# Seven half-block products in place of eight for the second FFN product of chunks 2 to 8

## The chip, the cores and the metric

The kernel runs on one core of a Trainium2 chip. A core has five engines with an instruction queue each: TensorE (PE in the profile; PEld are its weight loads), VectorE (DVE), ScalarE (ACT), GpSimd (POOL) and SyncE (SP), which here only issues DMAs. The engines work side by side and wait for each other by semaphores. Matmul results land in PSUM, eight banks of 512 f32 values in each of 128 partitions; everything else lies in SBUF.

The metric is the device time of one execution in microseconds, the median of several runs. Less is better.

## The reference

An attention with 8 batches, 8 heads, 576 positions and 64 dimensions a head, in which half of the heads see a plain window of 32 positions ("plain") and half see every fourth of the last 128 ("dilated"); its output, as 4608 tokens of 512 values, goes through a gated FFN:

```python
def _moe_ref(x, w_gate, w_val, w_out):
    g = x @ w_gate                                   # 4608 x 512 @ 512 x 1536
    gelu = 0.5 * g * (1.0 + erf(g * inv_sqrt2))
    val = x @ w_val
    return (gelu * val @ w_out).astype(np.float32)   # 4608 x 1536 @ 1536 x 512
```

Inputs and output are f32; the kernel multiplies in f16 and accumulates in f32.

## The kernel before

The 4608 tokens are worked off in nine chunks of 512 tokens, c = 0 to 8. Each has two stages.

The **gate stage** computes, for twelve blocks nb of 128 columns of d_ff, the gate product and the value product (ffn1_part, L617, 4 matmuls of 512 columns each) into two pairs of PSUM banks that alternate; from chunk 2 on blocks with even nb use banks 0 and 7, those with odd nb 1 and 4. ScalarE makes g = gelu(gate) (L776), VectorE u = USCALE * g * value (L781), written as block nb of the tile u_all (128 x 12 x 512, f16).

The **out stage** is the second product, u @ w_out: for four blocks of 128 tokens twelve matmuls of 512 columns (ffn2, L624), into banks 0 and 7 in turn in chunks 1 to 6. Each result is evicted by VectorE or ScalarE with a factor 1/USCALE (store, L635 and L637) to one of four buffers osb and stored by a DMA issued on SP (L639). The fourth of a chunk (e3) is evicted by ScalarE at the head of the next gate stage. The very last block of the kernel is cut in 384 and 128 columns (last_block, L648 to L660).

In chunks 1 to 6 the attention of the next batch is woven into the out stage, four head pairs i, j, k, l of it. Per pair: S, the scores, on TensorE (L452); P, the exponentials, on ScalarE (L482); M, the mask, on VectorE (L487); D and N, denominator and numerator, on TensorE (L452); l and r, the reciprocal by logarithm and exponential, on ScalarE (L579, L585); X, numerator times reciprocal into xT, on VectorE (L608). xT is what the gate stages of the next chunks read. For batches 2 and 3 the dilated pairs are i and j, for later ones k and l.

GpSimd turns loaded f32 into f16: for a batch the casts of q and k (cast_plain L211, cast_dil L223) and of v (cast_v L248, called by cast_part). The inputs of a batch are loaded on SP two chunks ahead: load_first loads q and k and emits their casts; load_rest emits DMA transposes (turn, L266) and the loads of v (load_v, L235 to L244). The v casts of batches 5 to 7 are emitted by the words v0 and v1 in the out stage, behind a mask (word M); those of batch 4 by load_rest(4) itself.

The order on every engine is written out by hand: gate_words(c) and out_words(c) give a string of words, run_program emits them one after the other, and each engine takes its instructions in that order. A number n emits the next n matmuls of the stage's product; g and u the two steps of a block; e and w evictions; F, H and R loads (F b is load_first(b), H b is load_rest(b), R stands at the head of chunk 2's gate stage and is load_rest(3), load_first(4), load_rest(4)); E and G load ScalarE's tables. The list of matmuls of a gate stage starts with an order by hand (orders, firsts), in which the parts that need the last X of the batch come at the tenth place from chunk 3 on.

Of the kernel before, what the change touches and what calls it, by code (L numbers as in the profile page):

```python
# [9 lines left out]
F16 = mybir.dt.float16  # L10
F32 = mybir.dt.float32
AF = mybir.ActivationFunctionType
ALU = mybir.AluOpType
# [1 line left out]
SYNC = mybir.DependencyInfo(mybir.DependencyClass.Sync, mybir.DependencyReason.DATA)  # L15
WIN = 32
DIL = 4
USCALE = 32.0


@with_exitstack
def kernel(
# [10 lines left out]
    nc = tc.nc  # L33
    B, H, S, D = q.shape
    NT, DM = out.shape
    DFF = moe_w_gate.shape[1]
    P = 128
# [49 lines left out]
    s16 = const.tile([P, 4608], F16, tag="s16")  # L87

    u_all = const.tile([P, NNB, CH], F16, tag="u")

    ps = psum.tile([P, 8, 512], F32, tag="ps")
    psf = ps.rearrange("p b c -> p (b c)")
# [472 lines left out]
            emit_tiles((mms, odd(n)))  # L565

    def two_t(n):
        dt = nrm.tile([P, 18, 32], F32, tag="dt", bufs=1)
        c0 = tiles["den", n]
        nc.vector.transpose(dt.rearrange("p b c -> p (b c)"), psf[:, c0 : c0 + S])  # L570
        rc = nrm.tile([P, 18], F32, tag="rc")
        nc.vector.reciprocal(rc, dt[:, :, 0:1].rearrange("p b c -> p (b c)"))
        tiles["rc", n] = rc
# [64 lines left out]
        t0 = c * CH + tb * P  # L638
        nc.sync.dma_start(out=out[t0 : t0 + P, :], in_=osb)  # L639

    def last_block(c, tb, bank):

        osb = osbp.tile([P, DM], F32, tag="osb")
        t0 = c * CH + tb * P
        for half in range(2):
            cs = slice(384 * half, 384 + 128 * half)
            for fc in range(NNB):
                nc.tensor.matmul(  # L648
                    ps[:, bank + 2 * half - 2, cs],
                    u_all[:, fc, tb * P : (tb + 1) * P],  # L650
                    wo_t[fc // 4][:, fc % 4, cs],
                    start=(fc == 0),
                    stop=(fc == NNB - 1),
                )
            src = ps[:, bank + 2 * half - 2, cs]
            if half:
                nc.vector.tensor_scalar(osb[:, cs], src, 1.0 / USCALE, None, ALU.mult)  # L657
            else:
                nc.scalar.activation(osb[:, cs], src, AF.Copy, bias=0.0, scale=1.0 / USCALE)
            (nc.scalar if half else nc.sync).dma_start(out=out[t0 : t0 + P, cs], in_=osb[:, cs])  # L660

    def warm(n, bank, rows=P, cols=CH):

# [60 lines left out]
    def gate_banks(c, nb):  # L724
# [21 lines left out]
    def out_list(c, banks):  # L746
        order = [(tb, fc) for tb in range(4) for fc in range(NNB)]
        if c == 0:
            order[: 3 * NNB] = [(tb, 4 * i + fc) for i, tbs in enumerate((range(3), range(3), (2, 1, 0))) for tb in tbs for fc in range(4)]
        return [lambda tb=tb, fc=fc: ffn2(c, tb, banks[tb], fcs=(fc,)) for tb, fc in order]  # L750

    def out_banks(c):
        if c == 0:
            return (0, 1, 2, 1)
        return (0, 7, 0, 7) if c < 7 else (2, 3, 5, 6)

    def run_program(c, words, mms, banks):
# [3 lines left out]
        for word in words.split():  # L761
# [20 lines left out]
            elif kind in "ew":  # L782
                at = args[1] if len(args) > 1 else c
                store(at, args[0], out_banks(at)[args[0]], "act" if kind == "e" else "dve")
            elif kind == "L":
                mms.clear()
                last_block(c, 3, banks[3])
# [18 lines left out]
    def gate_words(c):  # L806
# [7 lines left out]
            )  # L814
        loads = {1: "F3", 2: "R", 3: "F5 H5", 4: "F6 H6", 5: "F7 H7"}.get(c, "")
        rest = " ".join(f"4 g{nb} 4 u{nb}" for nb in range(2, NNB - 1))
        if c == 1:
            return f"{loads} 8 G 3 g0 1 u0 3 g1 1 u1 {rest} 4 g{NNB - 1} 4"
        before = f"e3@{c - 1}" if c < NCH - 1 else ""
        return f"{before} {loads} 7 G 3 g0 1 u0 1 g1 4 u1 {rest} 4 g{NNB - 1} 4" + (f" u{NNB - 1}" if c > 6 else "")  # L820

    def out_words(c):

# [8 lines left out]
        v0, v1 = (" v0", " v1") if 2 < c < 6 else ("", "")  # L832
        first = f"1 u11 4 S{i}@1+S{j}@4 E P{i} P{j} M{i} M{j} 7 w0 5" if c < 3 else f"E P{i} P{j} 1 u11 M{i} M{j}{v0} 12 w0 3"
        after = f"S{l + 1}@12+S{l + 2}@15" if 1 < c < 6 else ""
        return (
# [49 lines left out]
```

## Time and profile before

| what | value |
|---|---|
| median of 3 runs | 327.05 us (326.82 to 327.45) |
| profiled execution, first to last instruction (span) | 325.3 us |
| granted TensorE clock, mean | 1.000 |
| out stage of chunk 3 (144.9 to 158.2 us): TensorE, VectorE, ScalarE, GpSimd busy | 13.30, 7.83, 9.12, 2.29 us |
| gate stage of chunk 4 (158.2 to 178.9 us): the same | 20.70, 8.60, 8.98, 5.40 us |
| DMA issues to out_dram on SP | 35 of 256 KB and one of 192 KB |

The profile gives for its own execution the span alone; what a timed run has around its first and last instruction is the difference between the two, 1.75 us by the median.

Line numbers (L624) are those of the kernel before. A row of a group reads: line, engine, operation, output <- inputs, shapes and types, count, then busy time in all and the mean of one in ns, then the engine's idle time just before these instructions and what ended it. A row of the timeline reads: start, length (us), engine, line, operation, count, and in brackets the idle time before it and its releaser. In the timeline a row can merge several instructions. SPq is the issue of a DMA on SP's queue. A matmul row's length contains the pipeline's fill; its pace is the distance of starts.

### The profile page before, as it was taken

To read this page: it belongs to the slowest core of one execution; us is meant where nothing else is said; L and a number is where in the kernel's file an instruction comes from. 1 tells how busy PE (TensorE), PEld (TensorE's weight loads), DVE (VectorE), ACT (ScalarE), POOL (GpSimd) and SP (SyncE) were. 2 spreads that over 40 slices of the span, in tenths; PEclk is the share of its full clock that TensorE was granted. 3 is DMA by queue.
4 is the path that set the end of the run, shared out by engine and by line. 5 is a ranking of instruction groups with operands and counts; after the bars stand their busy time and mean duration, and the time that the engine had idled before them with its cause. 6 is when DMAs were issued, how large, how long until landed. Compare 5 with 4: busy or idle time off the path is not lost.

```text
span 325.3 us, 7737 instructions
## 1 busy us (share of the span) xinstructions
PE 318.9 (98%) x3207; PEld 155.8 (48%) x3207; DVE 150.2 (46%) x226; ACT 159.6 (49%) x240; POOL 82.3 (25%) x134
## 2 busy tenths in 40 slices
PE   6999999999999999999999999999999999999996
PEld 4754544445444445445444544445444544444443
DVE  6864636444644464346533554355434644204410
ACT  2662577435753556346633863376435753233321
POOL 8785603402482512332033201411000000000000
PEclk9999999999999999999999999999999999999999
DMA  8999998988799999897489537972000200020002
GB/s 190 188 188 206 201 191 165 269 180 199 171 271 208 240 169 245 197 222 191 119 201 232 141 104 157 253 173 90 32 2 8 94 33 0 2 99 30 0 34 97
DMA packets 106659, 47.11 MB, mean 145 GB/s; under 512 B 83584, under 2 KB 102144, under 8 KB 106624
## 3 DMA queue, kind: packets, MB, share of 16 engines
q1 hardware_dynamic: 93120, 38.29, 50.0%
q0 software_dynamic: 12944, 7.67, 16.7%
q10 hardware_dynamic: 560, 0.66, 0.7%
q8 instruction: 25, 0.41, 0.6%
q14 instruction: 10, 0.08, 0.1%
HBM read 37.75 MB, written 9.44 MB: 145 GB/s over the span
## 4 chain that ended last, share of the span: by engine, by line
PE 61%; ACT 0%; DVE 0%; issue 0%; ACTq 0%
PE ps L617 38%; PE ps L624 19%; PE ps L452 3%; PE ps L648 1%; ACT lg L579 0%; DVE osb L657 0%; ACTq L579 0%
## 5 line engine op out<-in xcount | busy, mean ns | idle before, releaser
L781 DVE SCALAR_TENSOR_TENSOR u_all<-g,ps 128x512 f16<-128x512 f16 x108 | 74.2, 688 | 110.0 <-PE ps L617 93.3
L776 ACT ACTIVATE g<-ps 128x512 f16<-128x512 f32 x108 | 63.6, 597 | 104.1 <-PE ps L617 104.1
L617 PE MATMUL ps<-xT,wg 128*128 128x512 f16 x432 | 112.5, 379 | 0.3 <-DMA wg<-in_moe_w_gate_dram 0.3
L617 PE MATMUL ps<-xT,wv 128*128 128x512 f16 x432 | 112.3, 379 | 0.0
L624 PE MATMUL ps<-wo,u_all 128*128 128x512 f16 x420 | 96.3, 380 | 0.0
L617 PEld LDWEIGHTS <-wv 128*128 128x128 f16 x432 | 42.1, 98 | 51.1 <-DMA wv<-in_moe_w_val_dram 0.7
L617 PEld LDWEIGHTS <-wg 128*128 128x128 f16 x432 | 42.1, 98 | 50.7 <-DMA wg<-in_moe_w_gate_dram 0.4
L624 PEld LDWEIGHTS <-u_all 128*128 128x128 f16 x420 | 39.1, 98 | 45.5 <-issue 0.5
L608 DVE TENSOR_TENSOR xT<-ps,rb 128x576 f16<-128x576 f32 x32 | 28.8, 938 | 16.9 <-PE ps L452 13.6
L482 ACT ACTIVATE P<-ps 128x832 f16<-128x832 f32 (+1 forms) x32 | 25.3, 835 | 15.4 <-PE ps L452 15.3
L211 POOL CAST s<-stage 128x640 f16<-128x640 f32 x24 | 17.4, 752 | 51.0 <-DMA stage<-in_q_dram 37.9
L248 POOL CAST v<-stage 128x1152 f16<-128x1152 f32 x11 | 12.7, 1151 | 63.0 <-DMA stage<-in_v_dram 47.4
L579 ACT ACTIVATE lg<-ps 128x576 f32<-128x576 f32 x30 | 18.7, 653 | 11.6 <-DVE xT L608 9.0
L637 DVE TENSOR_SCALAR osb<-ps 128x512 f32<-128x512 f32 x22 | 15.1, 686 | 12.2 <-PE ps L624 11.6
L585 ACT ACTIVATE rb<-lg 128x576 f32<-128x576 f32 x30 | 19.5, 690 | 0.3
L635 ACT ACTIVATE osb<-ps 128x512 f32<-128x512 f32 x13 | 7.8, 598 | 21.2 <-PE ps L624 21.2
L223 POOL CAST s<-stage 128x512 f16<-128x512 f32 x24 | 14.4, 627 | 10.1 <-DMA stage<-in_q_dram 7.9
L487 DVE TENSOR_TENSOR P<-P,two_d 128x768 f16<-128x768 f16 x14 | 9.4, 678 | 9.8 <-ACT P L482 9.1
L487 DVE TENSOR_TENSOR P<-P,two_p 128x832 f16<-128x832 f16 x14 | 8.6, 612 | 9.5 <-ACT P L482 9.5
L803 ACT ACT_TABLE_LOAD x9 | 11.5, 1283 | 0.2
L452 PEld LDWEIGHTS <-v 64*64 64x64 f16 x616 | 7.6, 107 | 6.3 <-issue 5.7
L452 PEld LDWEIGHTS <-q 64*64 64x64 f16 x576 | 7.9, 107 | 5.0 <-issue 3.0
(67 smaller groups left out, 135.6 us busy)
## 6 DMA issues: line engine op xcount, KB each, us to landing
out_dram<-osb SPq DMA_DIRECT2D x35, 256.0 KB, 2.8
stage<-in_v_dram SPq DMA_DIRECT2D x28, 144.0 KB, 3.8
stage<-in_q_dram SPq DMA_DIRECT2D x24, 128.0 KB, 3.6
stage<-in_k_dram SPq DMA_DIRECT2D x24, 128.0 KB, 2.9
stage<-in_q_dram SPq DMA_DIRECT2D x6, 512.0 KB, 4.7
stage<-in_k_dram SPq DMA_DIRECT2D x6, 512.0 KB, 5.3
stage<-in_v_dram SPq DMA_DIRECT2D x20, 128.0 KB, 2.8
wo<-in_moe_w_out_dram POOLq DMA_DIRECT2D x3, 512.0 KB, 16.8
```

The lines of the kernel that those rows point to most:

```text
L211: nc.gpsimd.tensor_copy(s16[:, 1280 * t + 640 * g : 1280 * t + 640 * g + 640].rearrange("p (k c) -> p k c", k=5), st_of(i).rearrange("p (k ...
L452: nc.tensor.matmul(o[cols], lhs[rows], rhs[rows], start=st, stop=end, skip_group_check=True)
L482: nc.scalar.activation(pt[:, 0 : src.shape[1]], src, AF.Exp, bias=0.0, scale=scale)
L487: tiles["M"] = nc.vector.tensor_tensor(pt, pt, mask, ALU.mult)
L579: nc.scalar.activation(lg, psf[:, c0 : c0 + S], AF.Ln)
L585: nc.scalar.activation(rb, tiles.pop(("lg", n)), AF.Exp, scale=-1.0)
L608: nc.vector.tensor_tensor(dst, num, rb, ALU.mult)
L617: nc.tensor.matmul(ps[:, bank, :], w[:, kc, ns], xT[kc][:, tok], start=first, stop=end)
L624: nc.tensor.matmul(ps[:, bank, :], u_all[:, fc, tb * P : (tb + 1) * P], wo_t[fc // 4][:, fc % 4, :], start=(fc == 0), stop=(fc == NNB - 1),)
L637: nc.vector.tensor_scalar(osb, ps[:, bank, :], 1.0 / USCALE, None, ALU.mult)
L776: nc.scalar.activation(g, ps[:, gate_banks(c, args[0])[0], :], AF.Gelu)
L781: nc.vector.scalar_tensor_tensor(u_all[:, nb, :], tiles.pop(("g", nb)), USCALE, val, ALU.mult, ALU.mult)
```

## The change

The second product of chunks 2 to 8 is computed by Strassen's scheme. Per pair j of u blocks (2j, 2j+1) and for the two halves of 256 tokens, A is the 2 x 2 arrangement A11, A21 (block 2j, tokens 0 to 255 and 256 to 511), A12, A22 (block 2j+1); B the same of w_out: k = block of the pair, h = half of the 512 output columns. Seven products replace eight: M1 = (A11+A22)(B11+B22), M2 = (A21+A22)B11, M3 = A11(B12-B22), M4 = A22(B21-B11), M5 = (A11+A12)B22, M6 = (A21-A11)(B11+B12), M7 = (A12-A22)(B21+B22). Each is 6 pairs x 2 blocks of 128 tokens = 12 matmuls of 256 columns into one bank.

Word by word: K (weight_sums) makes the sums of w_out once, in chunk 1's gate stage, on VectorE. k (u_sums) makes the sums of u, three instructions per pair, behind every second u word, on VectorE; the differences overwrite u. The products go to two banks in the order M3, M4, M5, M1, M2, M7, M6, where M5 adds to M3's bank, M1 and M7 to M4's. q0, q1, q3 take snapshots M3, M4 and M4+M1 (f32, in SBUF); q2, q4, q5, q6 write the four quarters of the output. s0, s1, s2 (part_sum) are sums between snapshots: f += m3, m3 = q2's quarter - m3, f -= q4's quarter; q5 reads m3, q6 reads f. Their engine is GpSimd in chunks 2 to 7; in chunk 8 s0 and s2 are on VectorE. The number behind the second @ of q and s names the engine (q: 1 ScalarE, 0 VectorE; s: 1 VectorE, 0 GpSimd). The eviction e3 at the head of the next gate stage goes away for these chunks; q6 is emitted at the end of the out stage, ahead of X{l}. The last product is split for the end (last_products). USCALE becomes 16, and the small tile dt of two_t becomes the fixed tile turned, whose place is a snapshot later.

```diff
-USCALE = 32.0
+USCALE = 16.0
...
+    NKP, HM = NNB // 2, DM // 2
+    ux = const.tile([P, NKP, 3, 2 * P], F16, tag="ux")
+    wx = [const.tile([P, 4, 2, HM], F16, tag=f"wx{i}", name=f"wx{i}") for i in range(3)]
+    t3s = [xT[i][:, 0:CH].rearrange("p (j d) -> p j d", j=2) for i in range(3)]
+    turned = const.tile([P, 18 * 32], F32, tag="turned")
+    snap = [vdiag.bitcast(F32)[:, DM * i : DM * i + DM] for i in range(2)] + [turned[:, 0:DM]]
...
-        dt = nrm.tile([P, 18, 32], F32, tag="dt", bufs=1)
+        dt = turned.rearrange("p (b c) -> p b c", c=32)
...
+    def weight_sums(i, part):
+        w = wo_t[i].rearrange("p (j k) (h d) -> p j k h d", k=2, h=2)
+        b11, b12, b21, b22 = (w[:, :, k, h] for k in range(2) for h in range(2))
+        if part == 0:
+            nc.vector.tensor_tensor(wx[i][:, 0], b11, b22, ALU.add)
...
+        elif part == 2:
+            nc.vector.scalar_tensor_tensor(wx[i][:, 2], b21, -1.0, b22, ALU.mult, ALU.subtract)
...
+    def u_sums(j, part):
+        k0, k1 = u_all[:, 2 * j, :], u_all[:, 2 * j + 1, :]
+        if part == 0:
+            nc.vector.tensor_tensor(ux[:, j, 1:3].rearrange("p s t -> p (s t)"), k0, k1, ALU.add)
+        elif part == 1:
+            nc.vector.tensor_tensor(ux[:, j, 0], k0[:, 0:256], k1[:, 256:512], ALU.add)
+        else:
+            two = u_all[:, 2 * j : 2 * j + 2, :]
+            flat = two.rearrange("p k t -> p (k t)")[:, 256:768].rearrange("p (k t) -> p k t", k=2)
+            nc.vector.tensor_tensor(flat, two[:, :, 256:512], two[:, :, 0:256], ALU.subtract)
...
+    def products(bank, kind, first):
+        return [
+            lambda s=s, t=t, p=p, st=first and j == 0 and p == 0, end=j == NKP - 1: nc.tensor.matmul(
+                ps[:, bank, HM * p : HM * p + HM], s[:, P * p : P * p + P], t, start=st, stop=end, skip_group_check=True
+            )
+            for j, (s, t) in enumerate(operands(kind))
+            for p in range(2)
+        ]
+
+    def seven(banks):
+        order = ((1, 3, True), (0, 4, True), (1, 5, False), (0, 1, False), (1, 2, True), (0, 7, False), (1, 6, True))
+        return [mm for b, kind, first in order for mm in products(banks[b], kind, first)]
+
+    def part_out(c, what, eng, banks):
+        src, by = ps[:, banks[0 if what in (1, 3, 5) else 1], :], 1.0 / USCALE
+        m3, a, f = snap
+        dst = {0: m3, 1: a, 3: f}.get(what)
...
+        if what < 4:
+            if eng:
+                nc.scalar.activation(dst, src, AF.Copy, bias=0.0, scale=by)
             else:
+                nc.vector.tensor_scalar(dst, src, by, None, ALU.mult)
+        else:
+            other, op = {4: (a, ALU.add), 5: (m3, ALU.subtract), 6: (f, ALU.add)}[what]
+            nc.vector.scalar_tensor_tensor(dst, src, by, other, ALU.mult, op)
...
+            dram = out[t0 : t0 + 256, d0 : d0 + HM].rearrange("(p r) d -> r p d", r=P)
+            nc.sync.dma_start(out=dram, in_=osb.rearrange("r (p d) -> r p d", p=2))
+
+    def part_sum(what, eng):
+        m3, a, f = snap
+        e = nc.vector if eng else nc.gpsimd
+        if what == 0:
+            e.tensor_tensor(f, f, m3, ALU.add)
+        elif what == 1:
+            e.tensor_tensor(m3, tiles["O", 2], m3, ALU.subtract)
+        else:
+            e.tensor_tensor(f, f, tiles["O", 4], ALU.subtract)
+
+    def last_products(c):
+        for p, c0, c1, bank in ((0, 0, HM, 3), (1, 0, P, 5), (1, P, HM, 6)):
...
+    SEVEN = range(2, NCH)
...
+        sums = [""] * NNB
+        if c in SEVEN:
+            for j in range(NKP - 1):
+                sums[2 * j + 1] += f" k{j}@0 k{j}@1 k{j}@2"
+        if c == min(SEVEN) - 1:
+            for i in range(3):
+                for part in range(5):
+                    sums[1 + (5 * i + part) * 2 // 3] += f" K{i}@{part}"
...
-        before = f"e3@{c - 1}" if c < NCH - 1 else ""
+        before = f"e3@{c - 1}" if c < NCH - 1 and c - 1 not in SEVEN else ""
...
         if c > 6:
-            return "12 e0 12 e1 12 e2 12 w3" if c < NCH - 1 else "12 e0 12 e1 12 e2 L"
+            tail = "12 q6@0" if c < NCH - 1 else "L"
+            return f"12 q0@1 12 q1@1 12 q2@0 12 q3@1 s0@{c - 7} s1@0 12 q4@0 s2@{c - 7} 12 q5@0 {tail}"
...
+        if c in SEVEN:
+            ahead = c > 2
+            open_ = f"E P{i} P{j} 1 u11" if ahead else f"1 u11 7 S{i}@1+S{j}@4 E P{i} P{j}"
+            after = f"S{l + 1}@12+S{l + 2}@15" if 1 < c < 6 else ""
+            return (
+                f"{open_} k5@0 k5@1 {11 if ahead else 4} q0@0 M{i} M{j}{v0} k5@2 12 q1@1 8 S{k}@1+S{l}@4 D{i}@11+D{j}@41 4 q2@0 "
+                f"P{k} P{l} M{k} M{l}{v1} 12 q3@0 s0@0 s1@0 l{i} l{j} r{i} r{j} 12 q4@0 s2@0 N{i}@10+N{j}@40 D{k}@12+D{l}@42 "
+                f"X{i} X{j} 12 q5@0 6 l{k} r{k} l{l} r{l} N{k}@13+N{l}@43 {after} X{k} 6 q6@0 X{l}"
+            )
```

More of the change, by code (lines that the diff above doesn't have):

```diff
@@ L639, in store @@
         nc.sync.dma_start(out=out[t0 : t0 + P, :], in_=osb)
[L641 to L657, printed above, removed]
-            else:
-                nc.scalar.activation(osb[:, cs], src, AF.Copy, bias=0.0, scale=1.0 / USCALE)
-            (nc.scalar if half else nc.sync).dma_start(out=out[t0 : t0 + P, cs], in_=osb[:, cs])
+    def weight_sums(i, part):
[4 more added lines that the diff above has]
+        elif part == 1:
+            nc.vector.tensor_tensor(wx[i][:, 1], b11, b12, ALU.add)
+        elif part == 2:
+            nc.vector.scalar_tensor_tensor(wx[i][:, 2], b21, -1.0, b22, ALU.mult, ALU.subtract)
+        elif part == 3:
+            nc.vector.tensor_tensor(t3s[i], b12, b22, ALU.subtract)
+        else:
+            nc.vector.tensor_tensor(wx[i][:, 3], b21, b11, ALU.subtract)
@@ L746, in out_list @@
     def out_list(c, banks):
+        if c in SEVEN:
+            return seven(banks)
         order = [(tb, fc) for tb in range(4) for fc in range(NNB)]
@@ L784, in run_program @@
                 store(at, args[0], out_banks(at)[args[0]], "act" if kind == "e" else "dve")
+            elif kind == "k":
+                u_sums(*args)
+            elif kind == "K":
+                weight_sums(*args)
+            elif kind == "q":
+                part_out(c, args[0], args[1], banks)
+            elif kind == "s":
+                part_sum(*args)
             elif kind == "L":
                 mms.clear()
[L787 removed]
+                last_products(c)
             elif kind == "V":
```

42 lines of the change are left out of this document (39 added, 3 removed).

## The prediction

> **What bounds the kernel now.** I read the page's busy times first, then the chain that ended last, then that chain in order of time.
>
> ```profile
> span 325.3 us, 7737 instructions
> PE 318.9 (98%) x3207; PEld 155.8 (48%) x3207; DVE 150.2 (46%) x226; ACT 159.6 (49%) x240; POOL 82.3 (25%) x134
> PE 61%; ACT 0%; DVE 0%; issue 0%; ACTq 0%
> ...
> 145.05 3.45 PE ps L624 x16
> 148.50 0.85 PE ps L452 x64
> 149.35 2.91 PE ps L624 x13
> 152.26 0.88 PE ps L452 x63
> 153.14 3.13 PE ps L624 x14
> 156.27 0.90 PE ps L452 x79
> 157.16 1.19 PE ps L624 x5
> 158.35 20.72 PE ps L617 x96
> ...
> 280.75 10.36 PE ps L624 x48
> ...
> 319.60 2.63 PE ps L648 x24
> ```
>
> TensorE has no gap: the pieces are start, length, line, count, and each begins where the one ahead ended. A gate stage (L617) is 96 matmuls in 20.72 us, a second product alone (L624) 48 in 10.36 us; both are 0.2158 us for 512 columns. In chunks 2 to 6 an out stage is the second product with three bursts of attention (L452) laid in, 13.3 us in all. So a matmul less is time less, as long as the other engines still deliver on time. VectorE and ScalarE are half busy; GpSimd (POOL) is idle three quarters of the time, but that average hides what it waits for.
>
> **What goes.** Per chunk, 48 products of 512 columns become seven half-block products of 12 matmuls of 256 columns, 84 in all. Before has no 256-column matmul; the nearest rows are the last block, 12 of 384 columns and then 12 of 128, each with its own weight load:
>
> ```profile
> 320.90 1.33 PE ps L648 x16
> ```
>
> The 24 of L648 hold 12 x 512 = 6144 columns in 2.63 us, 0.428 ns a column; the last 16 (4 of 384, 12 of 128, 3072 columns) take 1.33 us, 0.433. So even 128-column matmuls hide their weight loads. At 0.428 a 256-column matmul is 0.1096 us and 84 are 9.20 us; the bounds are 9.06 (0.2158 halved) and 9.31 us (0.433). The gain is 1.16 us a chunk (1.05 to 1.30). Chunk 8 (78 of 256, 12 of 128 columns) goes from 7.77 + 2.63 = 10.40 to about 9.2 us. Seven chunks: 8.2 us, if nothing else moves.
>
> **What is added on VectorE.** The nearest rows to the sums (two f16 inputs in SBUF) are the masks; to the recombinations, the evictions.
>
> ```profile
> L487 DVE TENSOR_TENSOR P<-P,two_d x14: 547/558/1274, 43.3 to 252.9; 128x768 f16<-128x768 f16 x14
> L487 DVE TENSOR_TENSOR P<-P,two_p x14: 591/593/858, 46.1 to 249.8; 128x832 f16<-128x832 f16 x14
> ...
> L781 DVE SCALAR_TENSOR_TENSOR u_all<-g,ps 128x512 f16<-128x512 f16 x108 | 74.2, 688 | 110.0 <-PE ps L617 93.3
> L637 DVE TENSOR_SCALAR osb<-ps 128x512 f32<-128x512 f32 x22 | 15.1, 686 | 12.2 <-PE ps L624 11.6
> ```
>
> From 547 ns at 768 and 591 at 832 the step is 0.69 ns an element; 512 come to about 0.4 us and 256 to 0.25. The three u sums of a pair of blocks cost 0.4 + 0.25 + 0.4 = 1.05 us. In the gate stage, two blocks last 8 x 2 x 0.2158 = 3.45 us, in which VectorE works 2 x 0.69 + 1.05 = 2.4 us: covered, by more than a microsecond. The fifteen weight sums in chunk 1, three per two blocks at 0.4 to 0.7 us, are covered too. The maxima (1274, 858) bound the case that such a sum runs while GpSimd holds it up: one such delay fits, and costs nothing. Without that cover a late u would hold its bank and the next gate block.
>
> The seven evictions replace four. Each is 0.69 us, while a product lasts 12 x 0.1096 = 1.31 us, and the products alternate between two banks, so a read has one product to finish. In an out stage from chunk 3 on I lay VectorE out, in us from its first matmul: u11 to 1.0, k5 sums to 1.75, q0 to 2.5 (M5 wants its bank at 2.6), masks to 3.75, q2 at 5.75, masks to 7.2, q3 to 7.95, q4 to 8.65. No matmul up to there waits more than 0.1 us. The end of the stage does: q6 now stands in front of X{l}, the last of the normalizations that give the next chunk its xT.
>
> ```profile
> 153.22 1.42 DVE L608 TENSOR_TENSOR xT<-ps,rb 128x576 f16<-128x576 f32 x2 [1.00 <-PE ps L452]
> 157.07 2.16 DVE L608 TENSOR_TENSOR xT<-ps,rb 128x576 f16<-128x576 f32 x2 [1.58 <-PE ps L452]
> ```
>
> A dilated X is 1.08 us, a plain one 0.71. M6 ends at 12.1; q6 runs to 13.0 and X{l} to 14.05, and the tenth matmul of the next gate stage, its first reader, is due at 12.1 + 9 x 0.2158 = 14.04. That costs 0 to 0.2 us after chunks 3 to 5. After chunk 6, where no S burst lies between, it costs 0.3. In chunk 8 VectorE also does two f32 sums; its three last evictions queue, and the end comes 0.2 us later than it would.
>
> Edits with one answer, nothing: USCALE, the new home of dt, and the four stores of 256 KB a chunk in rows of 1 KB instead of 2 KB, which stand where stores stood on SP. The cover of the stores is that nobody waits for them but osb's four buffers, a chunk later; if SP needs 0.3 us more for each, the next q loads start up to 0.6 us later. ScalarE loses the eviction e3 at the head of a gate stage and gets q1, between P{j} and P{k}, where it sat idle; P{k} waits for its S burst anyway.
>
> **The three sums on GpSimd are the step that decides.** In chunks 2 to 6 the words s0, s1, s2 put part_sum on GpSimd, and q5 on VectorE reads what s1 left. Until q5 has read bank 0, gate block 0 of the next chunk, which writes bank 0, can't start. GpSimd takes its instructions in the order in which they are emitted. In chunk 2 the word R at the head of the gate stage emits load_rest(4), which ends with two casts of batch 4's v (cast_part, L248). They stand ahead of s0. When do they run?
>
> ```profile
> 114.63 0.29 POOL L291 COPY q<-q 128x128 f16<-128x128 f16 x1
> 122.84 1.15 POOL L248 CAST v<-stage 128x1152 f16<-128x1152 f32 x1 [7.92 <-DMA stage<-in_v_dram]
> 128.00 1.15 POOL L248 CAST v<-stage 128x1152 f16<-128x1152 f32 x1 [4.01 <-DMA stage<-in_v_dram]
> ...
> 121.30 2.66 SPq L235 DMA_DIRECT2D stage<-in_v_dram  x4
> 124.06 2.82 SPq L639 DMA_DIRECT2D out_dram<-osb  x4
> 126.93 2.27 SPq L204 DMA_DIRECT2D stage<-in_q_dram  x4
> ...
> 124.16 1.46 PE L617 MATMUL ps<-xT,wg 128*128 128x512 f16 x6
> ```
>
> The second cast waits for a DMA and ends at 129.15, while TensorE begins chunk 3 at 124.16. Now nothing on GpSimd is due there, so the lateness costs nothing; in the changed kernel it is in the path. Nothing in the change brings those loads forward: their issues stand ahead of chunk 2's stores on SP.
>
> The price of one sum (two f32 inputs, 512 elements) has no row; the nearest are these.
>
> ```profile
> L133 POOL TENSOR_TENSOR two_d<-late_of,class_of 64x64 f16<-64x64 f16 x2 | 0.6, 286 | 0.1
> L336 POOL COPY two_p<-band 64x64 f16<-64x64 f16 x2 | 0.5, 234 | 0.0
> L223 POOL CAST s<-stage 128x512 f16<-128x512 f32 x24 | 14.4, 627 | 10.1 <-DMA stage<-in_q_dram 7.9 <-DMA stage<-in_k_dram 2.3
> ```
>
> One input of 512 elements takes 0.63 us, the lower bound. A second input adds 52 ns at 64 elements; if that is all per element, 0.42 us at 512, so 1.05 us; twice a cast, 1.25 us, is the upper bound. I take 1.0, nearest to the only two-input row. The Trainium skill's GPSIMD Engine Reference (section 3.1, Elementwise) has about 2.6 cycles an element for a two-input op; by it, as an estimate, a sum would be 1.1 to 1.3 us and the total below some 0.4 us higher. No run here shows it yet.
>
> So: s0 from 129.2, s1 to 131.3, q5 to 132.1, and gate block 0 of chunk 3 at 132.2 instead of 124.16. That is **8.0 us late**, chunk 2's own gain being swallowed (bounds 7.2 with 0.63, 8.6 with 1.25). TensorE, done with chunk 2 at about 123, is idle for 9 us.
>
> **After the idle.** At the kernel's start the same 512-column matmul is seen slow:
>
> ```profile
> L665 PE MATMUL ps<-ones 128*128 128x512 f16 x4 | 1.6, 552 | 0.0
> ...
> 3.89 0.15 PEld L665 LDWEIGHTS <-ones 128*128 128x128 f16 x1 [0.28 <-issue]
> 4.31 0.15 PEld L665 LDWEIGHTS <-ones 128*128 128x128 f16 x1 [0.28 <-issue]
> ```
>
> There the weight loads are 0.42 us apart, half the pace of later, from TensorE's first work at 1.5 us to about 4.9, though the granted clock reads 1.00. Before shows no later idle, so whether 9 us of it bring the slow pace back is open: 0 us if not, half of 3.4 us = 1.7 if once, 3.4 if the way back takes twice as long. I take 1.7, the start's own length. The Trainium skill's TensorE: Matmul & The Clock Gate (Part 1, What's actually happening) says that about 3.4 us without work halve the clock and that about as long at work restores it; the start agrees, and by that rule the term stands.
>
> **Chunks 3 to 6.** There too s0 stands behind the last v cast of its chunk:
>
> ```profile
> 153.52 1.15 POOL L248 CAST v<-stage 128x1152 f16<-128x1152 f32 x1 [2.78 <-DMA stage<-in_v_dram]
> 185.75 1.15 POOL L248 CAST v<-stage 128x1152 f16<-128x1152 f32 x1 [2.14 <-DMA stage<-in_v_dram]
> 221.57 1.15 POOL L248 CAST v<-stage 128x1152 f16<-128x1152 f32 x1 [3.94 <-DMA stage<-in_v_dram]
> ...
> 159.39 2.13 SPq L204 DMA_DIRECT2D stage<-in_q_dram  x4
> 193.41 2.13 SPq L204 DMA_DIRECT2D stage<-in_q_dram  x4
> ```
>
> From a chunk's first q load to that cast it is 26.6, 26.4 and 28.2 us (126.93, 159.39, 193.41 to the casts). With the loads 1.6 us into the gate stage, behind q6's store, a chain of 27 us ends 27 - 19.1 = 7.9 us into the out stage, the cast at 9.05, s1 at 11.15, q5 at 11.9. Then X{k}, q6 and X{l} follow to 14.85, 0.8 us past the 14.04 above (0.2 at 26.4, 2.0 at 28.2). I take 0.8 each for chunks 4 and 5. In chunk 3 TensorE is slow at first and the loads catch up: 0.2. In chunk 6 nothing loads: 0.3, as above.
>
> **Sum.** 8.0 + 1.7 - 6 x 1.16 (chunks 3 to 8) + 0.2 + 1.6 + 0.3 + 0.2 (chunks 3, 4 and 5, 6, 8) = +5.0 us. The span goes from 325.3 to 330.3. The median of the runs, 327.05, is 1.75 above the profiled span; I leave that as it is: **332.0 us**.
>
> **The rivals.**
> 1. *The stall comes, the slow pace doesn't.* For: the granted clock never leaves 1.00. Against: the start. 332.0 - 1.7 = 330.3. With the cheap sum (-0.8), chunks 4 and 5 at 0.2 each (-1.2) and the gain at its bound (6 x 0.14 = -0.8) it is 327.5.
> 2. *Faster: the sums come in time.* In chunk 2, M7 ends at about 120, so s1 must be done by then and the v cast by 118. If the loads or GpSimd's order were so, 327.05 - 8.2 + 2.3 (the small waits) = about 321. Against: the cast's 128.00, ten microseconds past that point, and an engine that takes its queue in order. This is also the case in which the emitted order isn't the order run.
> 3. *GpSimd is late in each chunk.* With 1.25 us a sum, or chains of 28 us, chunks 3 to 6 lose 1 to 2 us each instead of 2.1 together, and the slow pace lasts longer: 335 to 338.
>
> **How the numbers follow.** Forecast 0.55 (330.5 to 334), rival 1 0.22 (327.5 to 330.5), rival 2 0.11, rival 3 0.12. What a measurement of this kernel can tell from no change is about 0.2%, 0.65 us; the three runs lie that far apart. Faster is rival 2, 0.11; no change the lowest end of rival 1, 0.04; slower the rest, 0.85. The range runs from near rival 1's low end into rival 3's lower half, 328.0 to 336.0; rival 2 and the tail of 3 stay out.
>
> **What would show it.** In the changed profile: one TensorE gap of some 9 us near 123 to 132, ended by VectorE's q5, which itself waited for GpSimd; s0 right behind the cast near 129; pieces of 12 matmuls at 1.31 us; at the stall's end, gate matmuls 0.42 us apart for some 3 us, or not. If s0 runs before 120, or TensorE has no such gap, the forecast is wrong at its main step. If the 256-column matmuls take over 0.12 us, the gain was mis-sized.

## The result, and the profile after

The changed kernel takes **336.01 us** (median of four runs, 334.21 to 338.43) against 327.18 us for the kernel before on the same chip: a ratio of 1.0276, 95% interval 1.0226 to 1.0325. The change costs 9 us. The forecast of 332.0 us had the sign but not the size, and the result lies just above its range of 328.0 to 336.0. The profiled execution is the longest of the four, 338.43 us; its span of 336.6 stands 11.3 above the 325.3 of before. One execution of a later kernel, the one with all edits together, took 1133.84 us, its gate stages 78.8 us each at a granted clock of 1.00; the ranges below leave it out, and no run shows its cause.

The head of the page after:

```profile
span 336.6 us, 8413 instructions
PE 315.0 (94%) x3453; PEld 180.6 (54%) x3453; DVE 216.8 (64%) x392; ACT 159.1 (47%) x239; POOL 107.3 (32%) x153
PEclk9999999999999995899999999999999999999999
```

TensorE works 4 us less than before and the span is 11 us longer: 94% busy instead of 98%. In slices 16 and 17 of 40 (126 to 143 us) the granted clock falls to 0.5 and 0.8. Where TensorE loses its time stands in the chain of waits in order of time (start, length, what):

```profile
129.92 1.15 POOL v L254
131.06 1.23 POOL turned L736
132.36 1.27 POOL vdiag L738
133.66 0.70 DVE osb L724
134.40 22.57 PE ps L623 x96
...
169.81 20.87 PE ps L623 x96
...
204.57 20.56 PE ps L623 x94
...
239.44 20.56 PE ps L623 x94
...
272.99 20.57 PE ps L623 x94
293.55 9.17 PE ps L696 x84
302.72 20.72 PE ps L623 x96
...
333.20 0.29 DVE osb L750
```

The same gate stages in the chain of before (chunk 4's, at 158.35, stands in the prediction):

```profile
124.33 20.72 PE ps L617 x96
...
192.37 20.72 PE ps L617 x96
226.40 20.72 PE ps L617 x96
260.03 20.72 PE ps L617 x96
...
291.11 20.72 PE ps L617 x96
...
322.25 0.29 DVE osb L657
```

Read the two side by side: chunk 3's gate stage starts 10.07 us later than before, chunk 4's 11.46, chunk 8's 11.61, and the last eviction ends 10.95 us later (333.49 against 322.54). A row with 94 matmuls starts at the third of the stage, behind a wait, so those stages are compared by their ends (start plus length): chunk 5's ends 12.04 us later, chunk 7's 12.80. Nearly all of it is lost at one place, the end of chunk 2, where the chain leaves TensorE: the cast of batch 4's v on GpSimd, s0 (L736), s1 (L738), q5 (L724), then the gate stage. From there to the end of chunk 7's gate stage the kernel loses another 2.7 us instead of gaining, 1.85 of them in chunk 3's slow gate stage; only the two chunks without attention gain clearly.

The timeline of after at that place (start, length, engine, line, what; in brackets the idle time before and who ended it):

```profile
122.41 0.25 PE L458 MATMUL ps<-P,v 64*64 64x32 f16 x6 [0.40 <-ACT lg L585]
...
126.94 9.07 SPq L729 DMA_DIRECT2D out_dram<-osb  x4
...
133.66 0.69 DVE L724 SCALAR_TENSOR_TENSOR osb<-ps,vdiag 128x512 f32<-128x512 f32 x1 [12.26 <-POOL vdiag L738]
134.40 2.72 PE L623 MATMUL ps<-xT,wg 128*128 128x512 f16 x6 [10.61 <-DVE osb L724]
136.06 2.16 SPq L210 DMA_DIRECT2D stage<-in_q_dram  x4
```

VectorE stands idle for 12.26 us ahead of q5, until s1 on GpSimd is done, and TensorE 10.61 us until q5 is. SP's queue stands behind the stores that wait for q5 and q6, so the next batch's q loads start at 136.06 instead of 126.93. The wait delays the loads of the chunks behind it as well.

### The profile page after: what moved, and what is told of

It reads as the page before. It is cut to its first block, busy times and chain, and to the rows that moved or that the text cites. A ratio compares the mean times of both kernels' runs of the same rounds, so it can differ in the third digit from the quotient of the medians.

```text
span 336.6 us, 8413 instructions
## 1 busy us (share of the span) xinstructions
PE 315.0 (94%) x3453; PEld 180.6 (54%) x3453; DVE 216.8 (64%) x392; ACT 159.1 (47%) x239; POOL 107.3 (32%) x153
## 4 chain that ended last, share of the span: by engine, by line
PE 79%; DMA 10%; DVE 3%; SPq 3%; POOL 2%; ACT 1%; issue 1%; DVEq 0%; POOLq 0%; ACTq 0%
PE ps L623 53%; PE ps L696 14%; PE ps L630 6%; PE ps L458 5%; DMA stage<-in_v_dram 3%; DMA wv<-in_moe_w_val_dram 3%; DMA q<-s 2%; DMA u_all<-in_q_dram 2%; DVE xT L614 2%; ACT lg L585 1%; SPq L241 1%; DVE osb L724 1%; SPq L246 1%; SPq L272 1%; SPq L250 0%
## 5 line engine op out<-in xcount | busy, mean ns | idle before, releaser
L623 PE MATMUL ps<-xT,wg 128*128 128x512 f16 x432 | 114.3, 382 | 12.3 <-DVE osb L724 11.0
L696 PEld LDWEIGHTS <-u_all 128*128 128x128 f16 x324 | 30.8, 98 | 5.6 <-issue 0.4
L696 PE MATMUL ps<-wx,u_all 128*128 128x256 f16 x240 | 29.4, 273 | 0.0
L696 PEld LDWEIGHTS <-ux 128*128 128x128 f16 x252 | 24.2, 98 | 3.4
L736 POOL TENSOR_TENSOR turned<-turned,vdiag 128x512 f32<-128x512 f32 x6 | 7.6, 1270 | 56.9 <-ACT turned L719 28.5
L724 DVE SCALAR_TENSOR_TENSOR osb<-ps,vdiag 128x512 f32<-128x512 f32 x14 | 9.7, 690 | 22.6 <-POOL vdiag L738 18.9
L630 PE MATMUL ps<-wo,u_all 128*128 128x512 f16 x96 | 22.4, 380 | 0.0
L696 PE MATMUL ps<-wo,ux 128*128 128x256 f16 x168 | 21.5, 273 | 0.0
L666 DVE TENSOR_TENSOR ux<-u_all 128x512 f16<-128x512 f16 x42 | 20.0, 476 | 1.4
L672 DVE TENSOR_TENSOR u_all<-u_all 128x512 f16<-128x512 f16 x42 | 18.7, 446 | 0.0
```

What stands on the lines that cost most here:

```text
L623: nc.tensor.matmul(ps[:, bank, :], w[:, kc, ns], xT[kc][:, tok], start=first, stop=end)
L630: nc.tensor.matmul(ps[:, bank, :], u_all[:, fc, tb * P : (tb + 1) * P], wo_t[fc // 4][:, fc % 4, :], start=(fc == 0), stop=(fc == NNB - 1),)
L666: nc.vector.tensor_tensor(ux[:, j, 1:3].rearrange("p s t -> p (s t)"), k0, k1, ALU.add)
L672: nc.vector.tensor_tensor(flat, two[:, :, 256:512], two[:, :, 0:256], ALU.subtract)
L696: lambda s=s, t=t, p=p, st=first and j == 0 and p == 0, end=j == NKP - 1: nc.tensor.matmul(ps[:, bank, HM * p : HM * p + HM], s[:, P * p : ...
```

## The experiments

Two theories at the outset: the place of the v casts in GpSimd's queue, ahead of s0, costs the time (then moving sums or casts gives it back); or the sums and evictions themselves, wherever they stand, are too much for the out stage. The gain alone was to be seen in chunks 7 and 8. The medians of before lay between 327.04 and 327.22 in these comparisons.

| kernel | median, us | ratio to before, interval |
|---|---|---|
| chunks 7 and 8 alone | 325.90 | 0.9958 (0.9946 to 0.9971) |
| chunk 2's sums on VectorE | 330.25 | 1.0111 (1.0076 to 1.0146) |
| chunk 2's casts behind its sums | 331.16 | 1.0134 (1.0099 to 1.0169) |
| 190 matmuls in the gap | 337.12 | 1.0310 (1.0294 to 1.0326) |
| 370 matmuls in the gap | 338.40 | 1.0347 (1.0320 to 1.0373) |
| chunks 2 to 6: all sums on VectorE | 337.45 | 1.0319 (1.0272 to 1.0366) |
| second casts of chunks 3 to 5 behind too | 324.91 | 0.9942 (0.9919 to 0.9965) |
| and M6 whole ahead of N | 324.31 | 0.9919 (0.9904 to 0.9934) |
| and q6 ahead of X, gate order (ten runs) | 326.80 | 0.9975 (0.9943 to 1.0007) |
| M6 whole, both casts behind | 323.54 | 0.9892 (0.9877 to 0.9907) |
| all of these edits together | 321.48 | 0.9831 (0.9817 to 0.9844) |
| the same kernel again | 321.06 | 0.9813 (0.9797 to 0.9829) |

### The gain by itself

```diff
-    SEVEN = range(2, NCH)
+    SEVEN = range(7, NCH)
```

> The changed kernel with the seven products in chunks 7 and 8 alone; chunks 0 to 6 as before. Theory (the matmul gain is real: 84 of 256 columns at 0.109 us against 48 at 0.2158): chunk 7's second product takes 9.2 us instead of 10.36, chunk 8's about as much with 0.2 to 0.6 us more at the end; 327.2 - 1.2 - 0.7 = 325.0 to 325.4 us. Rival (weight loads or bank switches eat the gain): 327 us or more.

Measured 325.90 us, 1.3 us less than before; the forecast of 325.0 to 325.4 is missed by half a microsecond, for which the runs (325.45 to 326.02) show no reason. The chain of this kernel:

```profile
280.68 9.17 PE ps L696 x84
...
310.57 6.56 PE ps L696 x60
```

Chunk 7's product takes 9.17 us instead of 10.36: 1.19 us gained, 0.109 us for 256 columns. The 60 matmuls of chunk 8 keep that pace. Where no attention lies beside it, the scheme pays.

### Chunk 2: its sums off GpSimd, or its casts out of the way

The first takes s0, s1 and s2 of chunk 2 to VectorE; the second emits batch 4's two casts behind s2.

```diff
+            sv = 1 if c == 2 else 0
...
-12 q3@0 s0@0 s1@0 l{i}
+12 q3@0 s0@{sv} s1@{sv} l{i}
...
-12 q4@0 s2@0 N{i}@10
+12 q4@0 s2@{sv} N{i}@10
```

> The changed kernel with s0, s1 and s2 of chunk 2 alone on VectorE instead of GpSimd. Theory (the queue): the 10.6 us gap of TensorE ahead of chunk 3 comes from s0 standing behind batch 4's v casts on GpSimd, and the slow pace after it (1.85 us) from the gap. Then both go: 336.0 - 10.6 - 1.9 = 323.5 us, plus up to 2 us because three sums of 0.69 us now stand in front of chunk 2's X on VectorE: 323.5 to 325.5 us, below the kernel before. Rival (the gap is something else that ends near 134 us, such as the v data itself being needed): a gap of 8 us or more stays, over 333 us.

```diff
-        if b < 5:
+        if b < 4:
             for part in range(0 if by_pool else 2):
                 cast_part(b, part)
...
+            v2 = " v0 v1" if c == 2 else ""
...
-12 q4@0 s2@0 N{i}@10
+12 q4@0 s2@0{v2} N{i}@10
```

> The changed kernel with the sums left on GpSimd, but the two v casts of batch 4 emitted behind s2 of chunk 2 instead of in load_rest(4). Theory (the queue): the gap goes as in the run with the sums on VectorE, and nothing is put on VectorE: 323 to 324.5 us. Rival (GpSimd's sum is too slow, 1.26 us each): s1 ends 2.6 us after q3 whatever stands in the queue, and TensorE still waits 2 us or more ahead of chunk 3: 326 us or more.

Measured 330.25 and 331.16; both forecasts, 323.5 to 325.5 and 323 to 324.5, are missed. In both the gap at chunk 2 is gone: the gate stage starts at 125.57 with the sums on VectorE and at 123.58 with the casts behind. But both gain only about half of what chunk 2 had cost. The timeline of the first, at chunk 3's end:

```profile
156.61 1.15 POOL L254 CAST v<-stage 128x1152 f16<-128x1152 f32 x1 [1.22 <-DMA stage<-in_v_dram]
...
161.12 0.59 PE L623 MATMUL ps<-xT,wg 128*128 128x512 f16 x2 [1.82 <-DVE osb L724]
```

and of the second:

```profile
156.97 1.15 POOL L254 CAST v<-stage 128x1152 f16<-128x1152 f32 x1 [3.05 <-DMA stage<-in_v_dram]
...
161.46 0.84 PE L623 MATMUL ps<-xT,wg 128*128 128x512 f16 x2 [4.15 <-DVE osb L724]
```

The wait has moved one chunk on. TensorE arrives earlier, the loads do not, and the next cast stands ahead of the next s0. In the changed kernel chunk 3 didn't show this wait: behind the 10 us lost before it, its second cast (163.58) waited for a mask and not for a load.

### The slow pace after the gap

Small matmuls into unused columns of a bank, emitted behind M6's first half, work nothing that is read; first 190, then 370.

```diff
+    def filler(n):
+        for _ in range(n):
+            nc.tensor.matmul(psf[:, 1984:2048], ones[:, 0:P], ones[:, 0:64], start=False, stop=True, skip_group_check=True)
...
-X{k} 6 q6@0 X{l}
+X{k} 6{fill} q6@0 X{l}
```

> The changed kernel with 190 idle matmuls of 64 columns on TensorE at the end of chunk 2's out stage, into 64 PSUM columns that nothing reads. Theory (the idle brings the slow pace): the gap stays as it is, but the gate stage of chunk 3 takes 20.7 us instead of 22.6, the granted clock there is 1.00, and the time falls by 1.8 us to about 334. Rival (the first matmuls of chunk 3 are slow for want of data or because VectorE's X is late): the gate stage stays at 22.6 us and the time at 336.

> The changed kernel with 370 instead of 190 idle matmuls in chunk 2's gap; 190 took 5.9 us and left 4.8 us of idle, after which the granted clock was 0.50 all the same. 370 take 11 to 11.5 us, the whole gap. Theory (idle halves the clock): granted clock 1.00 in the gate stage of chunk 3, which takes 20.7 us; with the gap of about 11 us unchanged or up to 1 us longer, 333 to 335 us. Rival (the slow pace has another cause): 22.6 us or more for that gate stage, 336 us or more.

Measured 337.12 and 338.40. The 190 were too few: they lasted 5.94 us and left 4.76 us without work, and the gate stage behind took 23.52 us, 2.8 more than at full pace. That run decided nothing of its own question. Windows of three kernels (window, length, then busy time and count of TensorE, weight loads, VectorE, ScalarE, GpSimd, then granted clock, DMA share, GB/s); first the changed kernel:

```profile
129.00:134.40 5.40, 0.00 (x0) 0.00 (x0) 0.74 (x2) 0.00 (x0) 4.40 (x4) 0.50 0.22 76
134.40:136.00 1.60, 1.60 (x4) 0.55 (x4) 1.60 (x3) 0.00 (x0) 0.45 (x1) 0.50 0.43 154
136.00:138.00 2.00, 2.00 (x6) 0.73 (x5) 0.28 (x1) 0.00 (x0) 0.00 (x0) 0.54 0.68 194
138.00:150.00 12.00, 12.00 (x57) 5.49 (x56) 8.44 (x16) 4.67 (x8) 4.18 (x6) 1.00 0.95 200
```

with 190 matmuls in the gap:

```profile
134.00:138.00 4.00, 3.98 (x10) 1.47 (x10) 1.89 (x3) 0.00 (x0) 0.46 (x1) 0.50 0.56 167
```

with 370, its window and its chain:

```profile
134.00:138.00 4.00, 4.00 (x62) 2.52 (x59) 2.62 (x4) 0.39 (x1) 1.32 (x2) 1.00 0.44 141
```

```profile
135.41 20.72 PE ps L623 x96
```

With TensorE at work throughout, the clock stays at 1.00 and the gate stage takes 20.72 us instead of 22.57. So the slow pace comes of the idle time, and costs 1.85 us there. Yet the kernel isn't faster, and the forecast of 333 to 335 us is missed. Its stage starts 1.01 us later than in the changed kernel: the cast ahead of s0 starts 0.44 us later (130.36), and the last small matmul ends at 135.42, 0.6 us after q5. So the stage ends 0.84 us earlier, at 156.13. At the end of chunk 4's gate stage 0.20 us of that is left (190.48 against 190.68): chunk 3's second cast starts at 164.37, later than the 163.58 of the changed kernel, and q5 waits 2.11 us for s1 behind it. Behind a late transfer a faster stage is worth less than it saves; how much the slow pace costs the whole kernel, this run doesn't settle.

### All sums on VectorE

```diff
-12 q3@0 s0@0 s1@0 l{i} l{j} r{i} r{j} 12 q4@0 s2@0 N{i}@10
+12 q3@0 s0@1 s1@1 l{i} l{j} r{i} r{j} 12 q4@0 s2@1 N{i}@10
```

> The changed kernel with s0, s1 and s2 of chunks 2 to 6 on VectorE, casts where they were. Theory (the queue): no wait for GpSimd anywhere, but 2.1 us more on VectorE in each out stage, in which it is busy 9.3 of 12.8 us and whose end sets the stage: X{i} comes 2 us later, N{l} waits for l{l} 2 us longer; about 1.5 to 2 us a chunk against 0.5 to 0.8: 326 to 330 us, slower than with GpSimd freed of the casts (e5, 324.9). Rival (VectorE has the room, as its busy share says): 323 to 325 us.

Measured 337.45 us, as slow as the changed kernel: a miss for both sides. With no sum of chunks 2 to 6 on GpSimd no cast stands ahead of one, and still nothing is gained. The timeline at the ends of chunks 4 and 5, and two windows at the end of chunk 4:

```profile
192.78 0.23 PE L458 MATMUL ps<-P,v 64*64 64x96 f16 x2 [0.42 <-DVE xT L614]
...
194.77 0.43 PE L458 MATMUL ps<-P,v 64*64 64x80 f16 x25 [0.98 <-ACT lg L585]
...
226.57 1.58 DVE L738 TENSOR_TENSOR vdiag<-osb,vdiag 128x512 f32<-128x512 f32 x1
```

```profile
192.00:195.00 3.00, 1.16 (x47) 0.74 (x48) 1.98 (x4) 2.12 (x4) 0.00 (x0) 1.00 0.30 101
195.00:198.00 3.00, 3.00 (x67) 1.99 (x55) 1.74 (x3) 1.72 (x2) 0.00 (x0) 0.50 0.24 80
```

Three sums of 0.69 us stand ahead of the normalizations X{i} and X{j} on VectorE, ScalarE's l waits for X, TensorE's N for l. From 192 to 195 TensorE works 1.16 of 3 us, and then, without one long gap, the clock falls to 0.50 as well. With a v cast of GpSimd running beside it, s1 took 1.52 us in chunk 3 and 1.58 in chunk 5, s2 0.91 in chunk 4, against 0.69 alone. Each out stage of chunks 3 to 6 lasts about 14 to 16 us (181.90 to 197.35 for chunk 4) instead of 13.3. Two chunks show the price without a cast beside the sums. With chunk 2's sums on VectorE chunk 3's gate stage starts at 125.57, with the casts behind at 123.58, 2.0 us earlier; and chunk 6 here takes 1.4 us more than in the changed kernel (34.91 against 33.55 us, from the end of its gate stage to the end of the next). So at this place of VectorE's order the second theory holds: the sums don't fit there, and GpSimd is the better place for them if nothing stands in front. A later place on VectorE, for s2 above all, which only q6 needs, wasn't tried.

### The casts behind the sums in all chunks

```diff
+            v1, v2 = "", " v0 v1" if c == 2 else v1
```

(with batch 4's casts and the place of {v2} as above: the second cast of chunks 3 to 5 now follows s2, the first stays where it was).

> As the run with batch 4's casts behind s2 (331.2 us), and in chunks 3 to 5 the second v cast (word v1) behind s2 too. Theory (the queue, in each chunk): the waits of TensorE for q5 ahead of chunks 4 to 6 (1.8 us and more in the profile, up to 4.2 with the slow pace after it) go; s1 ends in time, and what is left of loss is the wait of the N burst for l{l} (0.5 us a chunk) and of the next gate stage for X (0.4 to 0.8 us): 324 to 325.5 us, faster than the kernel before. Rival (the loss in chunks 3 to 5 is VectorE's own length, the casts only mask it): 327 us or more.

Measured 324.91 us: 11.1 us less than the changed kernel, and faster than before. Every operation is the same as in the changed kernel; only the order on GpSimd is another. What is left of waits, from the list of what TensorE waited for (total us, times, longest), is

```profile
PE ps L458 <- ACT lg L585: 2.4, 5, 0.5
...
PE ps L623 <- DVE xT L614: 0.4, 1, 0.4
```

The first row is N waiting for l, once in each of chunks 2 to 6.

### M6, q6 and the gate's order

Three further steps on that kernel: all twelve matmuls of M6 ahead of the last N; q6 ahead of X{k}, with an order of the gate's matmuls that needs the last X later; and the first cast, v0, behind s2 too.

```diff
-X{i} X{j} 12 q5@0 6 l{k} r{k} l{l} r{l} N{k}@13+N{l}@43 {after} X{k} 6 q6@0 X{l}
+X{i} X{j} 12 q5@0 12 l{k} r{k} l{l} r{l} N{k}@13+N{l}@43 {after} X{k} q6@0 X{l}
```

> As e5, and all 12 matmuls of M6 ahead of the last N burst instead of 6 ahead and 6 behind. Theory (N{l} has to wait for l{l}, which waits for X{j}): the 0.5 us gaps inside the last N burst of chunks 2 to 6 go, but q6 and X{l} come no earlier, so part of it returns as a wait for X{l}: 0.5 to 1.5 us less than e5. Rival (the end of VectorE's chain, X{l}, sets the stage's length whatever TensorE does before): the same time as e5 within 0.3 us.

```diff
-N{k}@13+N{l}@43 {after} X{k} q6@0 X{l}
+q6@0 N{k}@13+N{l}@43 {after} X{k} X{l}
...
-        3: "000 001 002 100 101 102 010 011 012 003 013 103 110 111 112 113",
+        3: "000 001 010 011 002 012 100 101 102 003 013 103 110 111 112 113",
+        4: "002 003 012 013 000 010 102 103 100 001 011 101 112 113 110 111",
...
-    firsts = {c: orders[c if c < 3 else 2 if c == 3 else 3] for c in range(NCH)}
+    firsts = {c: orders[c if c < 3 else 4 if c == 3 else 3] for c in range(NCH)}
```

> As e6, with q6 ahead of X{k} on VectorE, and the next gate stage started with the eight matmuls (four before X{k} is needed) that need only the first two X. Theory (after the casts, the end of VectorE's chain against the gate stage's order is what is left): the waits for X at the gate stage's head shrink to under 0.3 us in chunks 2 to 5 and about 0.6 in chunk 6; 321 to 323 us. Rival (s2 on GpSimd, 4 us after q3, is now late for q6): the waits stay, named by GpSimd: 324 us or more.

```diff
-            v1, v2 = "", " v0 v1" if c == 2 else v1
+            v0, v1, v2 = "", "", " v0 v1" if c < 6 else ""
```

The last edit, once on the kernel with M6 whole and once with everything:

> As e6 (324.3 us), with both v casts of chunks 3 to 5 behind s2; VectorE's order and the gate order as in the changed kernel. Theory: only chunk 3's wait for the cast goes (1.3 us at the head of chunk 4's gate stage in e6's profile, with 0.5 behind it): 322.5 to 323.5 us; what e9 is below that is worth of its order of q6 and X. Rival: 324 us as e6.

> As e8 (322.9 to 330.0 us over its runs), and word v0, the first v cast of chunks 3 to 5, behind s2 too; no cast that waits for a load then stands ahead of a sum. Theory (e8's spread and chunk 3's wait in its profile, s0 at 153.4 right behind a cast at 152.3, are the same queue once more): no wait for GpSimd in chunk 3, the runs within 1 us of each other, 320.5 to 322 us. Rival (the spread comes from the loads by another way, such as a batch's q and k turned too late for S): a spread of 3 us or more stays.

> The same kernel as the run with both casts behind and the new gate order, again, for a profile of an ordinary execution. Theory (every wait that the change added stands on VectorE or GpSimd in the out stage, and the order of the gate's matmuls hides the last X): 321 to 322.5 us, no gap of TensorE over 1 us between two chunks, granted clock 1.00 in all windows, gate stages of chunks 3 to 6 at 20.7 us or up to 0.3 us less. Rival (the casts that now run behind s2 make the next chunk's loads late): a wait of GpSimd for stage buffers shows up at the queries of chunk 7, and chunk 7's gate starts over 31 us after chunk 6's.

M6 ahead of N took 0.6 us by the medians (the runs overlap): the waits of N vanish, and waits of the gate stage for X and q5 come instead:

```profile
PE ps L623 <- DVE xT L614: 2.4, 5, 0.8
...
PE ps L623 <- DVE osb L724: 1.3, 1, 1.3
```

Without a better order of the end most of the microseconds only change their place. q6 ahead of X with the new gate order, the first cast still in front of s0, is a miss: 326.80 us with runs from 322.92 to 330.01, though its profiled execution, a short one of 323.21, shows fewer waits. In it chunk 3's first cast still ran ahead of s0 (152.32), and the runs of each kernel with that cast behind lie within 0.8 us of each other. It fits that the loads' scatter reached s0 in the longer runs, and that their mean granted clock is 0.990 to 0.995, against 1.000 in the two shortest; none of those has a trace, so this isn't shown. With both casts behind, the median is 323.54 (forecast 322.5 to 323.5), and with the order too 321.48 and, again, 321.06. Page and waits of TensorE of that last run:

```profile
PE 311.8 (98%) x3453; PEld 180.2 (56%) x3453; DVE 213.8 (67%) x392; ACT 159.1 (50%) x239; POOL 107.0 (33%) x153
...
PEclk9999999999999999999999999999999999999999
```

```profile
...
PE ps L623 <- DVE xT L614: 0.3, 1, 0.3
```

TensorE is back at 98%, and of the waits at the chunks' ends 0.3 us is left. This version is 6 us faster than before and 15 us faster than the change as it was made. The bound of 31 us in that expectation was set too low: before already needs 33.63 us from chunk 6's gate stage to chunk 7's (226.40 to 260.03). This run needs 32.99 (223.33 to 256.32, counted from the same matmul), and no wait for a load stands there, so the rival of late loads is out.

## Why the prediction was wrong, and what of it was right

At chunk 2 the mechanism was as forecast, link by link: the second v cast of batch 4, s0, s1, q5, then bank 0's gate block, with one long gap of TensorE and a slow pace behind it. Two terms of the sum failed: the length of that wait, and chunks 3 to 6, in which a wait was put at nothing. The sizes, from the rows above against the prediction's terms:

| term | predicted | in the profile |
|---|---|---|
| start of chunk 3's gate stage | +8.0 | +10.07 |
| slow pace behind it | +1.7 | +1.85 |
| rest of chunk 3 | -0.96 | -0.31 |
| chunk 4 | -0.36 | +0.43 |
| chunk 5 | -0.36 | +0.84 |
| chunk 6 | -0.86 | -0.08 |
| chunk 7 | -1.16 | -1.19 |
| chunk 8 | -0.96 | -0.66 |
| sum | +5.0 | +10.95 |

From chunk 3 on, a chunk's term is the time from the end of its gate stage to the end of the next one (in chunk 8 to the last eviction), after less before; the own gain of 1.16 is in it. The profile is of the longest execution: by the medians the change costs 8.83 us, not 10.95. How the 2 us between are spread over the terms, no other trace shows.

- **The gain of the matmuls** was right: 1.19 us in chunk 7 against 1.16, and "at 0.428 a 256-column matmul is 0.1096 us" against 9.17 / 84 = 0.1092.
- **Chunk 2's wait, the first step that was mis-sized.** "s0 from 129.2, s1 to 131.3, q5 to 132.1": it was 131.0, 133.6 and 134.3, and the wait of 10.07 lies outside the bounds of 7.2 to 8.6. Of the 2 us, 1.9 are the cast, taken over from the trace of before at 128.00 and found at 129.92. The same cast started at 128.42 where chunks 2 to 6 were unchanged and at 129.5 to 130.4 in the runs with the gap, so the time of a DMA was used as if it were fixed. The last v loads were issued at 124.19 instead of 121.30, behind DMA transposes whose issue began 2 us later and took 9.15 us instead of 7.58; why, is open. The price of a sum adds half a microsecond (the two took 2.6 us instead of 2.1), of which shorter gaps between the steps take back 0.2:

```profile
L736 POOL TENSOR_TENSOR turned<-turned,vdiag 128x512 f32<-128x512 f32 x6 | 7.6, 1270 | 56.9 <-ACT turned L719 28.5
```

1.27 us, just above the upper bound of 1.25, where the prediction took 1.0. The estimate of 1.1 to 1.3 us from the Trainium skill's GPSIMD Engine Reference (section 3.1, Elementwise) agrees with the 1.27.

- **The slow pace** was right, 1.85 against 1.7, and the run with 370 matmuls shows the idle time to be its cause. That the size fits is in part luck: behind the gap of 4.76 us, less than half as long, it was 2.8. The Trainium skill's TensorE: Matmul & The Clock Gate (Part 1, What's actually happening) has 3.4 us without work as what halves the clock; the 4.76 us of the run with 190 did so. The run with all sums on VectorE, in which the clock fell behind idle pieces of 1 us at most, agrees rather with another section of that page of the Trainium skill, A second HAM failure mode: psum-queue depth-cycling, in which frequent short idles, there between groups of matmuls that cycle through PSUM banks, take the clock back too. What the prediction didn't see is that late loads behind the stage can take back what a faster one saves, 0.64 of 0.84 us in the run with 370.
- **Chunks 3 to 6, the second step that was mis-sized, and the larger**: -2.5 forecast, +0.9 found. The timeline of after, end of chunk 4:

```profile
199.01 1.15 POOL L254 CAST v<-stage 128x1152 f16<-128x1152 f32 x1 [3.33 <-DVE osb L724]
199.15 1.42 DVE L614 TENSOR_TENSOR xT<-ps,rb 128x576 f16<-128x576 f32 x2 [0.23 <-PE ps L458]
200.00 0.65 ACT L585 ACTIVATE lg<-ps 128x576 f32<-128x576 f32 x1 [1.26 <-DVE xT L614]
...
201.95 0.39 PE L458 MATMUL ps<-P,v 64*64 64x80 f16 x25 [0.51 <-ACT lg L585]
...
202.78 0.69 DVE L724 SCALAR_TENSOR_TENSOR osb<-ps,vdiag 128x512 f32<-128x512 f32 x1 [2.22 <-POOL vdiag L738]
...
204.57 1.02 PE L623 MATMUL ps<-xT,wg 128*128 128x512 f16 x4 [0.45 <-DVE xT L614]
```

The chain of loads was forecast well: the cast ends at 200.16, 9.5 us into the out stage, against 9.05. With sums of 1.27 us q5 ends at 12.8 instead of 11.9, and the first reader of X waits 0.45 us. But the larger part was left out: "No matmul up to there waits more than 0.1 us." That layout followed VectorE to q4 and not the chain through three engines behind it: X (199.15) waits for the burst with the first N, l on ScalarE (200.00) for X, and the second N (201.95) for the second l. From the start of X to the end of that l it is 2.75 us, as long as in the same chunk of before (187.25 to 190.00). There the matmuls of the product between the two bursts covered it, and the second burst follows without a gap (chain of before):

```profile
187.16 3.13 PE ps L624 x14
190.29 0.90 PE ps L452 x79
```

Now there are 18 matmuls of 256 columns between them, in 2.07 us, and N waits 0.4 to 0.5 us in every chunk from 2 to 6, off GpSimd altogether. The wait for X at the next gate stage comes on top. The experiments bear this out. From the end of chunk 3's gate stage to the end of chunk 7's, after needs 0.9 us more than before. With the second casts behind the sums it is 0.1 us less (144.48 to 280.10), with both casts behind and M6 whole 1.0 less (144.24 to 278.92), and with the new order of q6, X and the gate 3.2 less (143.88 to 276.34). So in these chunks the casts were the smaller part and the end of the out stage the larger. In chunk 6, which has no cast, the end cost 1.08 us (-0.08 against the own gain of 1.16), where the forecast had 0.3.
- **Rival 1** (no slow pace) is out, as the clock row shows. **Rival 3** came nearest, with late sums in each chunk at the bounds of their price, and its 335 to 338 us holds the result; it had 0.12. That its number fits is in part luck: it too put all the loss of these chunks on GpSimd. The forecast had set two uncertain terms at their favourable or middle values, where the rows that bore on them (a price with bounds 0.63 to 1.25, a DMA's time) were to be taken as a spread. **Rival 2** was false for this kernel, as argued. Its working, "about 321", is what the reordered version reached, 321.06, but that kernel has a new order of the end too; with the second casts out of the way and nothing else it was 324.91.
- Its counter-argument, "an engine that takes its queue in order", was the main matter: the emitted order of casts and sums on GpSimd makes 11.1 us of difference. Another 3.4 to 3.9 us came with both casts behind and the new order on TensorE and VectorE.

Open: why the four runs scatter by 4 us (334.21 to 338.43), since one of them has a trace.

## What to carry to other kernels

Before an operation whose end is waited for goes to an engine that is mostly idle, list what stands ahead of it in that engine's queue and what those wait for; an operation behind a DMA inherits the DMA's lateness and scatter. When such a wait is taken away, look where the late transfer shows up next: here it moved one chunk on, and only moving the casts in all chunks together brought the time below that of before. Where a change makes a product shorter, list what its length had covered, and follow that chain through all engines until it comes back to TensorE.

## What the runs showed of the hardware

- A gap of 4.76 us halved the granted clock (0.50) for about 5 us of work, and the gate stage behind it took 2.8 us longer; behind a gap of 10.61 us it was about 3.5 us of work and 1.85 us. But the clock also fell to 0.50 at 195 us in the run with all sums on VectorE, where TensorE had worked 1.16 of 3 us in pieces, and it stayed at 1.00 at the end of chunk 3 of the same run, where it had worked 1.39 of 3 us (156 to 159). What share of idle time in which window decides, these runs don't settle.
- A sum of two f32 tiles of 128 x 512 took 1.27 us on GpSimd and 0.69 on VectorE; with a cast of GpSimd beside it, 1.52 and 1.58 us on VectorE in two chunks.
- A matmul of 256 columns with a weight load of its own took 0.109 us, about as much a column as one of 512 (0.2158): halving the width cost some 1%.
